# An attention and MLP block on one core: loads of turned score rows, issued one piece per step behind a one-element write

## The chip, the cores and the metric

The kernel runs on one core of one Trainium2 chip. The metric is device time in microseconds (us) of one execution. The engines are named as in the profile: PE is TensorE, DVE is VectorE, ACT is ScalarE, POOL is GpSimd, and SP is SyncE, which here only issues DMA transfers.

## What is computed

The input x has 2048 rows of 448 numbers in float32. The reference, cut to what matters:

```python
xn  = layernorm(x)
q, k, v = xn @ wq, xn @ wk, xn @ wv      # 16 heads of 28 for q, one shared head for k and v
p   = softmax(q_h @ k.T * 28 ** -0.5)    # 2048 x 2048 for each head h
att = concat_h(p @ v) @ wo
y   = layernorm(xn)
mlp = gelu(y @ w1 + b1) @ w2 + b2        # 448 -> 1792 -> 448
out = x + att + mlp
```

## The kernel before, in words

The kernel has three stages. The first (to about 90 us) normalises x, projects q, k and v, and stores q to DRAM (`qd`). The second (to about 483 us) computes the MLP, 56 slots of `slot`; its sums with x are stored to the DRAM tensor `ad` (line 635). The third, which this change is about, is attention. The order of the work of each engine is the order of the program, written by hand: a queue does its instructions one after another, and one that waits holds those behind it.

**Units and steps.** The 2048 query rows are cut into 4 chunks of 512 (index c), the 16 heads into 4 groups of 4 (index g). A unit u is one chunk and one group, so there are 16 units. A step takes two of the 16 blocks of 128 key rows (index kt = 0, 2, ... 14), so a unit has 8 steps and the loop at line 873 has 128. Each step runs a string of letters from `ORDERS` (line 29). The ones that matter here:

- `s`: one `score` (line 849): a matmul of keys with queries (line 857) and the exponential of ACT into a tile `p` (line 858).
- `m`: one piece of `max_stream` (line 506). For every head but the turned ones of the next item, score rows are computed once ahead of time the other way round (line 516) to find each row's maximum, which DVE reduces (line 517). The queries for it, `qm`, are loaded by `load_m` (lines 429 to 436) in four small transfers per head, issued in the attention stage by POOL (`loads = pool`, line 875) shortly before the head before is finished.
- `t` and `x`: `turned_scores` (line 544) and `turned_exp` (line 563), the same work for the fourth head of units 1 to 15, which is computed with the query rows on the partitions. Its exponentials are stored to DRAM, `td[u]`, by SP (line 571), four stores of 256 KB for each tile of 128 query rows. Most of these stores lie in the MLP stage. The rest are in the attention stage, four in a unit.
- `T`: `turn_blocks` (line 838): DVE transposes 32 x 32 blocks of a `half` (line 840) and so gives the step the two `p` tiles of the fourth head.
- `P`: `pv` (line 821), twice a step: the matmuls of one key block's `p` tiles with the values (line 826), 16 instructions a step.
- `n`: a step of `norm_jobs` (line 751), which divides the finished unit by its row sums. It is a chain across queues: ACT copies `po` to `oc` (line 754), POOL issues rc<-oc (766), DVE takes the reciprocal (769), POOL issues ld<-rc to DRAM (770) and, when that has landed, tr<-ld (774), then multiplies (778) and splits the product into `oth` and `otl` (784, 785).
- `o`: a step of the output projection, `o_jobs` (line 731), in units 5, 9 and 13 and at the end. It adds to a row tile `a` that `load_rows_of` (line 726) has loaded from `ad`, and SP stores the sum to the output (line 744).
- `e`: `load_max` (line 492): the row maxima of the next unit go through PE, ACT and DVE and then, as two small transfers of POOL (lines 503 and 504, xh<-mn), into the queries of that unit.

**The loads around the change.** A unit's turned rows come back from DRAM as two `half` tiles of 2 MB each, the first for kt < 8, the second for the rest. `load_d(u, h)` (line 707) takes a new tile from a ring of three and issues the load of one half as four transfers of 512 KB, one for each quarter of the partitions, on SP's queue. In the program it stands at kt = 10 and 14 of the unit before (kt = 0 and 4 in unit 0). A transfer of SP waits only for what it needs: the data it reads, and the last reader of the buffer it overwrites. Nothing else ties it to the step at whose head it stands. `load_rows_of` loads single rows of the sum (`a`, ring of four, 224 KB each) on the same queue: one tile at every second step of `o_wait` (line 861), and all four of the last chunk at the step 14 before the end (line 877).

The lines that place them, of the loop over steps:

```python
if n == len(steps) - 14:
    load_rows_of(NCH - 1, range(CT))
if u + 1 < NU and kt in ((10, 14) if u else (0, 4)):
    load_d(u + 1, kt in (4, 14))
...
if u + 1 < NU and kt < 8:
    load_q(u + 1, (kt // 2,))
```

Of the kernel before, what the change touches and what calls it, by code (L numbers as in the profile page):

```python
# [8 lines left out]
F32 = mybir.dt.float32  # L9
# [6 lines left out]
P = 128  # L16
S, D, H, DH, F = 2048, 448, 16, 28, 1792
NT = S // P
CT = 4
# [19 lines left out]
def block_kernel(ctx, tc, x, wq, wk, wv, wo, w1, b1, w2, b2, out):  # L39
    nc = tc.nc  # L40
    pe, act, dve, pool = nc.tensor, nc.scalar, nc.vector, nc.gpsimd
# [12 lines left out]
    def heads_of(u):  # L54
        return 3 if u in TURNED else 4
# [6 lines left out]
    td = {u: dram.tile([32, 8, 4 * CT, 256], F32, name=f"td{u}") for u in TURNED}  # L62
# [361 lines left out]
    NU = len(units)  # L424
# [49 lines left out]
    def load_q(u, blocks=range(4)):  # L474
        c, g = units[u]
        cols = slice(c * CW, (c + 1) * CW)
        if u < 2 and 0 in blocks:
            qst.append(xt_p.tile([P, 4, CW], F32R, name="xh"))
            pool.memset(f(qst[u]), 0.0)
        qs = qst[u % 2]  # L480
        for b in blocks:
            blk, i = ((1, 0), (2, 0), (0, 1), (3, 1))[b]
            nh = heads_of(u)
            src = qd[i][4 * DH * g:4 * DH * g + DH * nh, cols].rearrange("(j r) n -> r j n", r=DH)
            loads.dma_start(f(qs[32 * blk:32 * blk + DH, 0:nh, :]), src)  # L485
        qss[u] = qs
# [5 lines left out]
    def load_max(u):  # L492
        qs, mr = qss[u], mrs.pop(u)
        nh = heads_of(u)
        pm = mtile([nh * CT, P])
        pe.transpose(pm, mr[:, 0:nh * CT], ident)
        mn = keep.tile([4 * CT, 2, P], F32R, name="mn", bufs=1)[0:nh * CT]
        if u:
            act.activation(mn[:, 0, :], pm, AF.Copy, scale=-1.0)
        else:  # L500
            dve.tensor_scalar(mn[:, 0, :], pm, -1.0, 0.0, op0=ALU.mult, op1=ALU.add)
        dve.scalar_tensor_tensor(mn[:, 1, :], pm, -1.0, f(mn[:, 0, :]), op0=ALU.mult, op1=ALU.subtract)
        loads.dma_start(f(qs[60:61, 0:nh, :]), f(mn[:, 0, :]))
        loads.dma_start(f(qs[124:125, 0:nh, :]), f(mn[:, 1, :]))
# [58 lines left out]
    def turned_exp():  # L563
        if not exps:
            return
        u, t, raw, m3, h = exps.pop(0)
        rs = slice(2 * h, 2 * h + 2)
        act.activation(raw[:, rs], raw[:, rs], AF.Exp, bias=m3[:, 4:5], scale=1.0)  # L568
        if h == 1:
            for a in range(4):  # L570
                nc.sync.dma_start(td[u][:, :, 4 * t + a, :],
                                  raw[32 * a:32 * a + 32].rearrange("p r (h b) i -> p (r h) (b i)", h=2))
            stored[u] = t
# [96 lines left out]
    for n in range(len(mslots) + 2):  # L670
        c, ft = mslots[n] if n < len(mslots) else (NCH, n - len(mslots))
# [28 lines left out]
    att = ctx.enter_context(tc.tile_pool(name="att", bufs=2))  # L700
# [3 lines left out]
    wor = att.tile([P, NG, D], F32, name="wor", bufs=1)  # L704
    halves = {}

    def load_d(u, h):
        assert stored[u] == CT - 1
        halves[u, h] = att.tile([P, 4 * CT, 256], F32, name="half", bufs=3)
        for r in range(4):  # L710
            nc.sync.dma_start(halves[u, h][32 * r:32 * r + 32], td[u][:, 2 * r + h, :, :])

    woh = att.tile([P, NG, D], F32R, name="woh", bufs=1)
    wol = att.tile([P, NG, D], F32R, name="wol", bufs=1)
# [5 lines left out]
    def prep_wo(g):  # L720
        act.activation(woh[:, g, :], wor[:, g, :], AF.Copy)
        pool.tensor_sub(wol[:, g, :], wor[:, g, :], f(woh[:, g, :]))

    rows = {}

    def load_rows_of(c, tiles):
        for k in tiles:
            rows[c, k] = keep.tile([P, D], F32, name="a", bufs=4)
            nc.sync.dma_start(rows[c, k], ad[:, CT * c + k, :])

    def o_jobs(c, gs, tiles=range(CT)):
        last = NG - 1 in gs
        for k in tiles:
            po = mtile([P, D])
            ts = slice(k * P, (k + 1) * P)
            for g in gs:
                oth, otl = ots[c, g]
                pe.matmul(po, oth[:, ts], woh[:, g, :], start=(g == gs[0]), stop=False)
                pe.matmul(po, oth[:, ts], wol[:, g, :], start=False, stop=False)
                pe.matmul(po, otl[:, ts], woh[:, g, :], start=False, stop=(g == gs[-1]))  # L740
            a = rows[c, k]
            dve.tensor_add(a, a, po)
            if last:
                (nc.scalar if k % 2 and c == NCH - 1 else nc.sync).dma_start(ov[:, CT * c + k, :], a)
            yield
# [75 lines left out]
    def pv(u, kt):  # L821
        if kt == 0:
            pos[u] = op.tile([P, CW], F32, name="po")
        po = pos[u]
        for j in range(4):
            pe.matmul(po[32 * j:32 * j + 32, :], vs[:, kt, :], ps.pop((u, kt, j)),  # L826
                      start=(kt == 0), stop=(kt == NT - 1))
        if kt == NT - 1:
            if u == NU - 1:
                end_jobs(u, pos.pop(u))  # L830
                return
            side.add(norm_jobs(u, pos.pop(u)))
            side.step()
            c, g = units[u]
            if c < NCH - 1 and g == NG - 1:
                oside.add(o_wait(c, range(NG), range(CT)))

    def turn_blocks(u, kt):
        p = pair_of()
        dve.transpose(p.rearrange("p k (g j) -> p g k j", j=32),  # L840
                      halves[u, kt // 8][:, :, 32 * (kt % 8):32 * (kt % 8) + 64].rearrange("p g (k j) -> p g k j", j=32))
        ps[u, kt, 3], ps[u, kt + 1, 3] = p[:, 0], p[:, 1]
# [6 lines left out]
    def score(u, kt, j):  # L849
        if not halfway:  # L850
            p = pair_of()
            halfway.append(p[:, 1])
            p = p[:, 0]
        else:
            p = halfway.pop()
        s = mp.tile([P, CW], F32, name="m")
        pe.matmul(s, ks[:, kt * P:(kt + 1) * P], qss[u][:, j, :], start=True, stop=True)  # L857
        act.activation(p, s, AF.Exp, scale=SCALE)  # L858
        ps[u, kt, j] = p

    def o_wait(c, gs, tiles):
        for k in range(4):
            load_rows_of(c, tiles[k:k + 1])
            yield
            yield
        yield from o_jobs(c, gs, tiles)
# [6 lines left out]
    for n, (u, kt) in enumerate(steps):  # L873
        if n == 0:
            loads = pool
        if n == len(steps) - 14:
            load_rows_of(NCH - 1, range(CT))
        if u + 1 < NU and kt in ((10, 14) if u else (0, 4)):
            load_d(u + 1, kt in (4, 14))
        if 4 <= n < 4 + NG:  # L880
            prep_wo(n - 4)
        if u + 1 < NU and kt < 8:
            load_q(u + 1, (kt // 2,))
        jobs = [(u, kt + k, j) for k in range(2) for j in range(heads_of(u))]
        for what in ORDERS[u in TURNED][n % 2]:
            if what == "s":
                score(*jobs.pop(0))
            elif what == "m":
                if maxed < total - left + left * sum(weight[:n + 1]) / sum(weight):
                    maxed += mxs.step()  # L890
            elif what == "t":
                tq.step()
            elif what == "x":
                turned_exp()
            elif what == "T":
                if u in TURNED:
                    turn_blocks(u, kt)
            elif what == "e":
                if kt == (6 if u + 2 < NU else 10) and u + 1 < NU:
                    load_max(u + 1)  # L900
            elif what == "n":
                side.step()
            elif what == "o":
                if n == len(steps) - 5:
                    oside.add(o_jobs(NCH - 1, range(NG - 1)))
                oside.step()
            elif what == "P":
                assert not jobs
                for _ in range(BURST if n else 0):
                    pv(*pvq.pop(0))  # L910
# [29 lines left out]
```

## Time and profile before

| What | Value |
|---|---|
| median of the three runs | 1127.99 us (1127.91 to 1135.29) |
| the profiled execution | 1129.17 us |
| its span, first to last instruction | 1127.4 us |
| mean granted clock of PE over the span | 0.991 |
| DMA moved | 195.13 MB, mean 173 GB/s |
| `half` loads | 120 transfers of 512 KB, SP |
| stores of `td` | 240 transfers of 256 KB, SP |

The profile is one execution on the chip. Its head gives each engine's busy time; its other views group instructions by line, list who waited for whom, follow the chain that ended last, or show instructions in order of time. In those rows a name such as qm<-qd says what was written from what, an arrow with "<-" in a list of waits names the releaser, and brackets in the view by time hold the idle time before an instruction and its releaser. A stretch's row has the busy time and the number of instructions of each engine, then the clock granted to PE (1.00 is full), the mean busy share of the 16 DMA engines and what they moved. "Us to landing" is the time from a transfer's issue until its data are there; it is given for transfers that POOL issued. SPq and POOLq are the queues of those engines.

### The profile page before, as it was taken

The page shows a single profiled execution, that of the slowest core. Times are in us where ns is not written, and L with a number is a line of the kernel's source. Part 1 is how long each engine was busy: PE and PEld are TensorE (multiplying, and loading weights), DVE is VectorE, ACT ScalarE, POOL GpSimd, SP SyncE. Part 2 cuts the span into 40 slices and gives each one's busy share as a digit, 9 for nine tenths or more (in the row PEclk, how much of TensorE's full clock was granted, in tenths as well). Part 3 has the DMA queues.
Part 4 walks back from the last instruction along what each step waited for, and adds up shares of the span by engine and source line. Part 5 has one row for each costly group of instructions (what it writes and reads, how often), then busy time and mean ns, then how long its engine had stood idle before and what let it go on. Part 6 is the DMA issues. An engine that isn't in the chain of part 4 may idle for free.

```text
span 1127.4 us, 17253 instructions
## 1 busy us (share of the span) xinstructions
PE 1089.9 (97%) x5777; PEld 717.0 (64%) x5777; DVE 905.8 (80%) x1711; ACT 736.6 (65%) x1279; POOL 553.3 (49%) x683
## 2 busy tenths in 40 slices
PE   9999999999999999999999999999999989979988
PEld 8768878888888888854555456555455444545444
DVE  7789889888898988976889886888877968857734
ACT  6765655666667665578677765777755767745764
POOL 6357777778777777934324415333433333233120
PEclk9999999999999999999999999999999989989989
DMA  8775445777777777685787693979676957846910
GB/s 274 208 218 152 132 128 159 184 181 189 205 178 191 185 197 196 165 212 127 169 191 178 161 217 118 229 167 222 170 155 172 219 133 182 220 101 143 219 40 33
DMA packets 113669, 195.13 MB, mean 173 GB/s; under 512 B 17070, under 2 KB 96100, under 8 KB 109740
## 3 DMA queue, kind: packets, MB, share of 16 engines
q1 hardware_dynamic: 100972, 172.34, 61.3%
q0 software_dynamic: 11200, 21.10, 7.6%
q8 instruction: 46, 0.75, 0.3%
q10 hardware_dynamic: 1408, 0.57, 0.2%
q14 instruction: 43, 0.35, 0.1%
HBM read 115.22 MB, written 77.71 MB: 171 GB/s over the span
## 4 chain that ended last, share of the span: by engine, by line
PE 56%; DMA 21%; issue 8%; POOL 7%; DVE 5%; ACT 1%; SPq 1%; POOLq 0%; DVEq 0%; ACTq 0%
PE m L516 10%; PE po L826 9%; PE ph L179 9%; DMA ld<-rc 8%; PE m L857 8%; DMA qm<-qd 4%; PE m L550 4%; DMA tr<-ld 4%; PE m L627 3%; PE m L624 3%; PE m L630 3%; POOL qm L434 2%; DMA td<-raw 1%; POOL xh L485 1%; POOL tr L774 1%
## 5 line engine op out<-in xcount | busy, mean ns | idle before, releaser
L517 DVE TENSOR_REDUCE mx<-m 128x1 f32<-128x512 f32 x784 | 506.0, 680 | 111.4 <-PE m L516 102.8
L858 ACT ACTIVATE p<-m 128x512 f32<-128x512 f32 x784 | 402.9, 610 | 175.7 <-PE m L857 175.6
L516 PE MATMUL m<-ks,qm 128*128 128x512 f32 x784 | 324.3, 414 | 13.6 <-DMA qm<-qd 11.1
L857 PE MATMUL m<-xh,ks 128*128 128x512 f32 x784 | 260.8, 403 | 7.5 <-DMA xh<-mn 5.2
L826 PE MATMUL po<-p,vs 128*32 128x512 f32 x2048 | 249.7, 606 | 0.0
L516 PEld LDWEIGHTS m<-ks,qm 128*128 128x128 f32 x784 | 147.8, 188 | 134.9 <-ACT p L858 45.0
L857 PEld LDWEIGHTS m<-xh,ks 128*128 128x128 f32 x784 | 146.7, 190 | 56.6 <-ACT p L858 12.9
L551 DVE TENSOR_SCALAR_CACHE_REDUCE raw<-m 128x512 f32<-128x512 f32 x240 | 159.8, 689 | 18.5 <-DMA td<-raw 7.2
L840 DVE STREAM_TRANSPOSE p<-half 128x1024 f32<-128x1024 f32 x120 | 148.0, 1235 | 5.7 <-PE po L826 3.3
L568 ACT ACTIVATE raw<-raw,m 128x1024 f32<-128x1024 f32 x120 | 133.0, 1150 | 0.6 <-DVE m L557 0.6
L826 PEld LDWEIGHTS po<-p,vs 128*32 128x32 f32 x2048 | 54.1, 110 | 124.0 <-issue 118.3
L598 ACT ACTIVATE hx<-ph,b1t 128x512 f32<-128x512 f32 x56 | 38.6, 690 | 138.1 <-PE ph L184 138.1
L550 PE MATMUL m<-ks,q 128*128 128x512 f32 x240 | 95.6, 399 | 4.5 <-DVE raw L551 2.4
L613 POOL TENSOR_TENSOR hl<-hx,hh 128x512 fp32r<-128x512 f32 x56 | 73.4, 1311 | 35.4 <-ACT hh L611 35.4
L774 POOL DMA_DIRECT2D tr<-ld x56 | 28.1, 507 | 114.7 <-DMA ld<-rc 114.7
L630 PE MATMUL m<-w2h,hl 128*128 128x448 f32 x224 | 82.9, 370 | 0.3 <-POOL hl L613 0.3
L627 PE MATMUL m<-w2l,hh 128*128 128x448 f32 x224 | 81.7, 365 | 0.0
L624 PE MATMUL m<-w2h,hh 128*128 128x448 f32 x224 | 81.6, 364 | 0.0
L606 POOL TENSOR_TENSOR hx<-hx,hz 128x512 f32<-128x512 f32 x56 | 74.3, 1328 | 4.7
L601 POOL TENSOR_TENSOR hz<-hz,hx 128x512 f32<-128x512 f32 x56 | 72.6, 1296 | 4.7
L179 PE MATMUL ph<-xh,w1h 128*128 128x512 f32 x168 | 66.2, 394 | 0.0
L179 PE MATMUL ph<-xh,w1l 128*128 128x512 f32 x168 | 65.8, 391 | 0.0
(164 smaller groups left out, 1335.1 us busy)
## 6 DMA issues: line engine op xcount, KB each, us to landing
td<-raw SPq DMA_DIRECT2D x240, 256.0 KB
half<-td SPq DMA_DIRECT2D x120, 512.0 KB
xh<-qd POOLq DMA_DIRECT2D x60, 168.0 KB, 4.3
a<-in_A_x_dram SPq DMA_DIRECT2D x32, 224.0 KB
qd<-qe SPq DMA_DIRECT2D x24, 256.0 KB
qm<-qd POOLq DMA_DIRECT2D x108, 56.0 KB, 4.0
qm<-qd SPq DMA_DIRECT2D x88, 56.0 KB
ad<-a SPq DMA_DIRECT2D x16, 224.0 KB
```

The costliest lines, as they stand in the source:

```text
L179: pe.matmul(ps, w, v, start=(n == 0), stop=False)
L516: pe.matmul(pm, qm[:, t * P:(t + 1) * P], ks[:, n * CW:(n + 1) * CW], start=True, stop=True)
L517: dve.tensor_reduce(mx[:, CT * j + t, n:n + 1], pm, axis=AX.X, op=ALU.max)
L550: pe.matmul(sc, q3[i][:, t * P:(t + 1) * P], ks[:, n * CW:(n + 1) * CW], start=True, stop=True)
L551: dve.tensor_scalar(raw[:, :, 4 * n:4 * n + 4, :].rearrange("p r b i -> p b r i"), sc.rearrange("p (b r i) -> p b r i", r=4, i=32), SCALE, ...
L568: act.activation(raw[:, rs], raw[:, rs], AF.Exp, bias=m3[:, 4:5], scale=1.0)
L627: pe.matmul(m2[k], hh[:, ts], w2l[:, ft, :], start=False, stop=False)
L630: pe.matmul(m2[k], hl[:, ts], w2h[:, ft, :], start=False, stop=(ft == NF - 1))
L826: pe.matmul(po[32 * j:32 * j + 32, :], vs[:, kt, :], ps.pop((u, kt, j)), start=(kt == 0), stop=(kt == NT - 1))
L840: dve.transpose(p.rearrange("p k (g j) -> p g k j", j=32), halves[u, kt // 8][:, :, 32 * (kt % 8):32 * (kt % 8) + 64].rearrange("p g (k j) ...
L857: pe.matmul(s, ks[:, kt * P:(kt + 1) * P], qss[u][:, j, :], start=True, stop=True)
L858: act.activation(p, s, AF.Exp, scale=SCALE)
```

## The change

`load_d` takes an index i from 0 to 7 in place of a half. Each call issues one of the eight pieces of a unit, and before it DVE writes one element of that piece (a zero at its first partition and column, which the load then overwrites). The load writes the same element, so it cannot be issued before DVE has come to that write. The call stands at the head of every step of units 0 to 14, i = kt / 2. The rows of the sum get the same write. No transfer changes its size, its queue or its number.

```diff
-    def load_d(u, h):
+    def load_d(u, i):
         assert stored[u] == CT - 1
-        halves[u, h] = att.tile([P, 4 * CT, 256], F32, name="half", bufs=3)
-        for r in range(4):
-            nc.sync.dma_start(halves[u, h][32 * r:32 * r + 32], td[u][:, 2 * r + h, :, :])
+        h, r = divmod(i, 4)
+        if r == 0:
+            halves[u, h] = att.tile([P, 4 * CT, 256], F32, name="half", bufs=3)
+        part = halves[u, h][32 * r:32 * r + 32]
+        dve.memset(part[0:1, 0, 0:1], 0.0)
+        nc.sync.dma_start(part, td[u][:, 2 * r + h, :, :])
...
     def load_rows_of(c, tiles):
         for k in tiles:
             rows[c, k] = keep.tile([P, D], F32, name="a", bufs=4)
+            dve.memset(rows[c, k][0:1, 0:1], 0.0)
             nc.sync.dma_start(rows[c, k], ad[:, CT * c + k, :])
...
-        if u + 1 < NU and kt in ((10, 14) if u else (0, 4)):
-            load_d(u + 1, kt in (4, 14))
+        if u + 1 < NU:
+            load_d(u + 1, kt // 2)
```

## The prediction

> **What bounds the kernel now.** I read the page's head first, then its list of transfers, then TensorE's waits in the attention stage, then that stage in slices, and last the queues around the slices that lose time. All views here are of the kernel before. The head and two transfers of the page:
>
> ```profile
> span 1127.4 us, 17253 instructions
> PE 1089.9 (97%) x5777; PEld 717.0 (64%) x5777; DVE 905.8 (80%) x1711; ACT 736.6 (65%) x1279; POOL 553.3 (49%) x683
> ...
> td<-raw SPq DMA_DIRECT2D x240, 256.0 KB
> half<-td SPq DMA_DIRECT2D x120, 512.0 KB
> ```
>
> TensorE (PE) is busy for 1089.9 of 1127.4 us, so what can be won without taking work away is its 37.5 us of idle time and the time in which it runs slowly. The change touches only the attention loop, from about 483 us on. The view of who waited for whom, for PE in 480 to 1127 us (total, times, longest):
>
> ```profile
> PE m L516 <- DMA qm<-qd: 11.1, 3, 5.7
> PE m L857 <- DMA xh<-mn: 5.2, 1, 5.2
> PE m L516 <- ACT p L858: 1.4, 2, 0.8
> PE m L740 <- POOL otl L785: 1.4, 2, 0.7
> PE m L857 <- ACT p L858: 1.3, 2, 0.7
> PE m L738 <- POOL oth L784: 1.2, 1, 1.2
> ```
>
> And the first two of its lines in order of time (start, duration, in brackets the idle time before):
>
> ```profile
> 513.72 0.47 PE L516 MATMUL m<-ks,qm 128*128 128x512 f32 x1 [2.59 <-DMA qm<-qd]
> ...
> 912.88 0.77 PE L516 MATMUL m<-ks,qm 128*128 128x512 f32 x1 [2.86 <-DMA qm<-qd]
> ...
> 995.45 0.77 PE L516 MATMUL m<-ks,qm 128*128 128x512 f32 x1 [5.68 <-DMA qm<-qd]
> ...
> 1078.95 2.90 PE L857 MATMUL m<-xh,ks 128*128 128x512 f32 x6 [5.21 <-DMA xh<-mn]
> ```
>
> Four waits for small transfers of POOL's queue make 2.59 + 2.86 + 5.68 + 5.21 = 16.3 us. The four lines of waits for ACT and POOL add 1.4 + 1.4 + 1.3 + 1.2 = 5.3 us. Elsewhere PE runs nearly without a gap, as the last row of the next fence shows for units 2 and 3 together, whose 16 transposes on VectorE (DVE) are in the row behind it. The stretches are those after the four stalls, one within a burst of loads, and the two units (columns: us; busy us and count of PE, PEld, DVE, ACT, POOL; granted clock; DMA share; GB/s):
>
> ```profile
> 514.00:528.00 14.00, 14.00 (x82) 7.08 (x81) 8.22 (x15) 12.22 (x23) 7.52 (x12) 1.00 0.20 59
> ...
> 912.88:920.00 7.12, 7.12 (x25) 3.18 (x26) 2.12 (x5) 1.33 (x3) 5.12 (x7) 0.56 0.04 13
> 995.45:1002.00 6.55, 6.55 (x24) 2.87 (x25) 1.38 (x2) 2.49 (x5) 5.51 (x9) 0.57 0.30 86
> 1078.95:1084.00 5.05, 5.05 (x22) 2.32 (x22) 0.00 (x0) 3.05 (x6) 2.85 (x3) 0.60 0.00 0
> ...
> 574.00:596.00 22.00, 22.00 (x132) 10.99 (x131) 19.27 (x32) 15.05 (x32) 5.62 (x11) 1.00 1.02 231
> ...
> 564.65:636.31 71.66, 71.66 (x426) 36.36 (x425) 63.76 (x103) 54.16 (x106) 23.12 (x39) 1.00 0.77 183
> ```
>
> ```profile
> L840 DVE STREAM_TRANSPOSE p<-half x16: 1222/1235/1241, 564.7 to 632.2; 128x1024 f32<-128x1024 f32 x16
> ```
>
> After each of the three later stalls the granted clock is 0.56 to 0.60 for some microseconds. The loss is 7.12 x 0.44 + 6.55 x 0.43 + 5.05 x 0.40 = 8.0 us, counted as busy time. After the first stall it stays at 1.00.
>
> Why are the small transfers late? The DMA queue of SP, in order of time:
>
> ```profile
> 486.46 5.03 SPq L711 DMA_DIRECT2D half<-td  x8
> 527.69 3.28 SPq L571 DMA_DIRECT2D td<-raw  x4
> ...
> 570.56 3.42 SPq L571 DMA_DIRECT2D td<-raw  x4
> 574.08 7.70 SPq L711 DMA_DIRECT2D half<-td  x8
> 606.42 3.46 SPq L571 DMA_DIRECT2D td<-raw  x4
> ...
> 961.55 3.17 SPq L571 DMA_DIRECT2D td<-raw  x4
> ```
>
> Four stores of td come once a unit, 12 times from 527.69 to 961.55 us. Unit 2 begins at 564.7 us. In the program its loads of `half` stand at the sixth and eighth step, but nothing holds SP back: once past the stores of td it issues all eight within 7.7 us, 4 MB behind 1 MB. The row 574 to 596 shows the DMA engines full (1.02) for 22 us at 231 GB/s. What that does to the small transfers, from the groups of lines 770, 774, 434 and 503 in this order (ld<-rc, tr<-ld, qm<-qd, xh<-mn):
>
> ```profile
> DMA to landing us min/median/max: 1.7/10.1/13.0
> DMA to landing us min/median/max: 2.1/6.3/10.4
> DMA to landing us min/median/max: 2.0/4.0/17.6
> DMA to landing us min/median/max: 1.6/9.6/14.2
> ```
>
> POOL's queue outside a burst, and before the stall at 989.8 us:
>
> ```profile
> 700.67 2.01 POOL L774 DMA_DIRECT2D tr<-ld  x4 [1.45 <-DMA ld<-rc]
> ...
> 974.70 0.58 POOL L770 DMA_DIRECT2D ld<-rc  x1 [4.07 <-DVE mx L517]
> 984.91 2.04 POOL L774 DMA_DIRECT2D tr<-ld  x4 [9.64 <-DMA ld<-rc]
> 986.95 2.01 POOL L434 DMA_DIRECT2D qm<-qd  x4
> ```
>
> For the same 8 KB POOL idles 1.45 us where SP sends little and 9.64 us in a burst (1.7 and 10 us from issue to landing). POOL waits for them in order, so the next qm (or xh<-mn) is issued late, and then is slow itself.
>
> **The change part by part.** *Holding the loads of `half`.* No transfer is added or taken away: 120 of 512 KB before and after. One goes out per step, behind a write that DVE does at the head of that step. Units 2 and 3 have 16 steps in 71.66 us, 4.48 us each. At 231 GB/s a piece takes 524 KB / 231 = 2.3 us, so SP's queue is empty for about half of most steps. Ahead of a small transfer there is at most one piece, or once per unit a piece and the four stores of td (1.05 MB, 4.5 us). My estimate for ld<-rc is therefore 2 to 4.3 us as a rule in place of 10.
>
> What that does to each stall: before 989.8 us POOL is released at least 9.64 - 4.3 = 5.3 us sooner, so the four qm are issued from 981.6 to 983.6 us and, with their group's median of 4.0, are there near 987.6, before PE runs dry. The stall that ends at 912.88 is a qm's too, and so is the one that ends at 513.72, behind eight loads issued from 486.46 on; the longest landing of the group is 17.6 us. With a piece ahead instead of a burst each should land over 5 us sooner (17.6 against 4.0 + 6.8), more than the 2.86 and 2.59 lacking. The last stall is xh<-mn's, which stands behind tr<-ld, which waited for ld<-rc; from the chain that ended last:
>
> ```profile
> 1059.34 9.50 DMA ld<-rc
> ...
> 1071.13 7.54 DMA xh<-mn
> ```
>
> With 4.3 and about 5 us in their place it lands 9.50 - 4.3 + 7.54 - 5 = 7.7 us earlier, against 5.21 us of stall. So I take all four: 16.3 us, and 8.0 us of slow clock with them. The bounds of this term are 0 (the waits stay) and 24.3.
>
> The small waits for ACT and POOL (5.3 us) stand at the end of the same chain, since `oc`, `oth` and `otl` wait for tr<-ld. Some are the ordinary meeting of two engines. Between 0 and 5.3 I take the middle, 2.7.
>
> The clock term can be read against a rule. In the Trainium skill, TensorE: Matmul & The Clock Gate, section "The HAM clock gate", the clock halves after an idle window of about 3.4 us and returns after a busy window of about 3.4 us. By that figure, an estimate from the page, three stalls would cost 3 x 1.7 = 5.1 us instead of 8.0, and the time would be 2.9 us longer. The trace differs on both counts: a stall of 2.86 us was enough, and a mean of 0.56 over 7.12 us means some 6 us at half.
>
> *The 120 one-element writes, and 16 for the rows.* The nearest row is a small memset of this kernel, and what hides it is DVE's idle time beside it:
>
> ```profile
> L382 DVE MEMSET vs<- x4: 62/62/62, 22.0 to 63.7; 128x4 f32 x4
> ```
>
> ```profile
> DVE mx L517 <- PE m L516: 7.7, 14, 0.8
> ```
>
> 136 x 0.062 = 8.4 us of DVE. In units 2 and 3 DVE idles 71.66 - 63.76 = 7.9 us in 16 steps, 0.49 us a step, 7.7 of it waiting for PE (the second fence, waits of 564 to 637 us): a write of 0.06 us fits eight times. Nothing is queued behind it but DVE's own next instruction, and it has nothing to wait for: the last readers of the buffer are DVE's own transposes of an earlier step. Bounds 0 and, doubled for the signalling, 17 us; I take 1, since PE is what DVE waits for.
>
> *SP's queue.* A piece now waits for DVE, and behind it stand td's stores of the same step (which wait for ACT, later in that step), stores of out, and rows: all belong to this step or later ones, so nothing is held longer than its step. Cost nothing.
>
> *Later loads.* The fourth piece of a half is issued in step 4 of unit u and first read in step 1 of unit u + 1, five steps or 22 us later; the eighth in step 8, read in step 5 of the next, the same. Piece and td's stores take 2.3 + 4.5 + 2 = 9 us. Cost nothing.
>
> *Rows of the sum.* 16 loads of 224 KB are held to steps in the same way, and are used five or more steps on. Their write needs the store that last read the buffer, whose issue is at least six steps back. Cost nothing, gain nothing.
>
> Sum: -16.3 - 8.0 - 2.7 + 1.0 = -26.0 us. The profiled execution took 1129.17 us (span 1127.4), so 1103.2; the median of the three runs, 1127.99, is 1.2 lower: 1102.
>
> **The rivals.** *A piece hurts as much as a burst.* If a small transfer's delay comes from there being any traffic of SP's and not from how much is queued, spreading makes the traffic omnipresent: per unit 4.2 MB of pieces and 1 MB of stores take 5.2 / 0.231 = 23 us of 35.8, so two thirds of the chances to be late stay, and 24.3 us shrink by a third: 1128 - 8 = 1120. For it: the ld<-rc of 974.70 us landed within 10 us, well before the last of the transfers that delayed qm behind it. Against it: the row 1.7 / 10.1 / 13.0, where the fast ones stand in stretches with some SP traffic too. The Trainium skill says in DMA: Bandwidth & Descriptors, "Queues, rings and completion order", that an engine goes round its queues packet by packet; by that the length of SP's backlog should not matter, and this rival would hold. No run here separates the two yet. Chance 0.15.
>
> *The write waits for the piece before it (slower).* If the writes of one `half` tile were ordered one behind another, DVE would stand at the head of each step until the last piece has landed. That takes 2.3 + 2.0 = 4.3 us, within the step's 4.48 + 0.49; but with td's stores ahead 8.8, which is 3.8 too many, in the 12 units that store: +46 - 24 = +22, 1150 us. It decides from a landing above 5 us on. Against it: the eight loads of 486.46, four to a tile, were issued in 5 us while a burst lasts 22, so parts of a tile were not ordered. Chance 0.08.
>
> *The stalls have another cause, or are replaced by the next late thing*, so that no more than a few us come of it: 1125 to 1130. For it: in most units the same slow chain stalls nothing, so the stalls need a coincidence that may come again elsewhere. Chance 0.09.
>
> *DVE becomes the bound*: at 0.11 us a step on the path, 128 steps cost 14 us, 1115. Against it, 0.49 us idle. Chance 0.06.
>
> **How the numbers follow.** The forecast, 1094 to 1110, has 0.62: its high end keeps one stall with its slow clock (5.68 + 2.8), its low end lets all of the 5.3 us go and the writes cost nothing (3.6 in all), and leaves 4 us for work stretched around the stalls that no row prices. With the DVE case (1111 to 1116) and a piece as bad as a burst (1112 to 1124) that makes 0.83; the range 1094 to 1126 takes in these three. One per cent, 11.3 us, is about what a measurement of this kernel can tell from no change. Faster by more: 0.62 + 0.06 + a third of 0.15 = 0.73. Within: 0.10 + 0.09 = 0.19. Slower: 0.08.
>
> **What would show it.** Right: eight loads of `half` some 4.5 us apart in SP's queue; the DMA share no longer 1.0 for 20 us and then 0; ld<-rc at a median under 5 us; no wait of PE for qm or xh<-mn above 1 us; granted clock 1.00 up to the last unit; units without rows of the sum near 36 us throughout. Wrong: ld<-rc still near 10 us (the first rival), a wait of DVE in front of the new writes (the second), or new waits of PE for `mx` (the last).

## The result, and the profile after

The changed kernel takes 1098.1 us at the median of four runs (1096.8 to 1102.2), the kernel before 1130.6 us beside it (1127.9 to 1135.3). The ratio is 0.971, 95% interval 0.967 to 0.976. The forecast was 1102 us, 26 us below the 1128.0 that was the median of before at the time. Against the medians of this comparison the change saves 32.5 us.

The profiled execution of the changed kernel took 1102.2 us with a span of 1100.4. It is the longest of the four, and some 3.5 us of it were lost before the code that changed: in the projection stage the clock was 0.83 from 60 to 80 us (1.00 in the profile of before), and the first score's matmul starts at 487.47 instead of 483.98 us. From that matmul to the end the kernels take 1127.4 - 484.0 = 643.4 us before and 1100.4 - 487.5 = 612.9 us after. So the attention stage is 30.5 us shorter, and that is the number to explain. The rows of the two stretches, before and after (columns as in the prediction):

```profile
483.98:1127.40 643.42, 617.01 (x3565) 323.77 (x3565) 483.13 (x760) 436.77 (x845) 211.82 (x340) 0.98 0.70 165
```

```profile
487.47:1100.40 612.93, 607.30 (x3565) 321.17 (x3565) 488.23 (x895) 437.05 (x845) 212.26 (x340) 1.00 0.74 173
```

PE's idle time fell from 643.4 - 617.0 = 26.4 us to 612.9 - 607.3 = 5.6, which is 20.8 us less, and its busy time by 617.0 - 607.3 = 9.7 us for the same 3565 matmuls.

The waits of PE from 480 us on, complete, in the changed kernel (its lines 861 and 742 are 857 and 738 of before):

```profile
PE m L861 <- DVE half L713: 1.0, 1, 1.0
PE m L742 <- ACT oth L812: 0.9, 1, 0.9
```

No wait for qm, xh<-mn, ACT's `p`, `otl` or `oth` of the norm chain is left. These two stand at the first score and at the end, and were there before too (waits for `a` and for `oth`). The reason shows in the landings of the same four groups as in the prediction (ld<-rc, tr<-ld, qm<-qd, xh<-mn):

```profile
DMA to landing us min/median/max: 3.8/4.3/7.4
DMA to landing us min/median/max: 2.1/4.1/6.5
DMA to landing us min/median/max: 2.1/4.6/11.7
DMA to landing us min/median/max: 1.7/5.5/7.3
```

The median of ld<-rc fell from 10.1 to 4.3 us. Its minimum rose from 1.7 to 3.8: in no unit does it find the way free any more, and in none does it stand behind a whole burst. For qm the median did not fall (4.0 before, 4.6 now); its longest did, from 17.6 to 11.7 us. SP's queue and the stretches answer to those shown of before; the stretches are the one that was a burst, the one that was idle, two whole units, and nearly all of the stage:

```profile
571.27 3.65 SPq L571 DMA_DIRECT2D td<-raw  x4
575.01 29.05 SPq L714 DMA_DIRECT2D half<-td  x8
607.12 3.58 SPq L571 DMA_DIRECT2D td<-raw  x4
```

```profile
574.00:596.00 22.00, 22.00 (x132) 10.96 (x131) 19.51 (x38) 15.05 (x31) 8.79 (x14) 1.00 0.81 199
600.00:604.00 4.00, 4.00 (x26) 1.93 (x25) 3.66 (x7) 3.13 (x7) 0.00 (x0) 1.00 0.77 181
565.35:637.01 71.66, 71.66 (x426) 36.33 (x425) 64.48 (x119) 54.16 (x106) 28.25 (x46) 1.00 0.77 186
490.00:1052.00 562.00, 562.00 (x3294) 295.99 (x3296) 466.92 (x864) 407.57 (x789) 207.19 (x336) 1.00 0.79 186
```

Of the kernel before, the row of the idle stretch is:

```profile
600.00:604.00 4.00, 4.00 (x26) 1.94 (x25) 3.36 (x6) 3.25 (x8) 3.71 (x5) 1.00 0.01 3
```

The eight loads now take 29 us to issue where they took 7.7. The DMA share is 0.81 where it was 1.02, and 0.77 where it was 0.01. From 490 to 1052 us PE is busy in all of 562.00 us at a clock of 1.00. Units 2 and 3 take 71.66 us, to the hundredth what they took before: the steady state has not become faster, only the stalls are gone.

### The profile page after: what moved, and what is told of

The parts are those of the page before. It is cut to its first block, busy times and chain, and to the rows that moved or that the text cites. A ratio compares the mean times of both kernels' runs of the same rounds, so it can differ in the third digit from the quotient of the medians.

```text
span 1100.4 us, 17517 instructions
## 1 busy us (share of the span) xinstructions
PE 1082.9 (98%) x5777; PEld 716.4 (65%) x5777; DVE 911.2 (83%) x1847; ACT 736.6 (67%) x1279; POOL 553.6 (50%) x683
## 4 chain that ended last, share of the span: by engine, by line
PE 89%; DVE 5%; DMA 3%; SPq 1%; ACT 1%; issue 1%; POOL 0%; ACTq 0%; DVEq 0%; POOLq 0%
PE po L830 22%; PE m L516 18%; PE m L861 17%; PE ph L179 9%; PE m L550 5%; PE m L630 4%; PE m L627 4%; PE m L624 4%; DMA qd<-qe 1%; DMA qm<-qd 1%; PE m L742 1%; PE m L743 1%; PE m L744 1%; PE ph L182 1%; PE ph L184 1%; DVE mx L517 1%
## 5 line engine op out<-in xcount | busy, mean ns | idle before, releaser
L830 PE MATMUL po<-p,vs 128*32 128x512 f32 x2048 | 246.0, 598 | 0.0
L861 PEld LDWEIGHTS m<-xh,ks 128*128 128x128 f32 x784 | 144.7, 188 | 50.0 <-ACT p L862 12.8
L179 PE MATMUL ph<-xl,w1h 128*128 128x512 f32 x168 | 66.3, 395 | 0.0
```

Source lines behind the costliest of these rows:

```text
L179: pe.matmul(ps, w, v, start=(n == 0), stop=False)
```

## The experiments

Each kernel is timed against the kernel before on the same chip.

### The new places without the write

The change with both writes taken out, so that the loads stand one per step but nothing holds SP.

```diff
-        dve.memset(part[0:1, 0, 0:1], 0.0)
...
-            dve.memset(rows[c, k][0:1, 0:1], 0.0)
```

> The change without its one-element writes: the eight loads of a unit stand one per step in the program, but nothing holds SP to the step. Theory 1 (small transfers are late by what SP has queued in front of them, and it is the hold that keeps this short): SP runs ahead as before, the eight loads go out within 8 to 10 us behind td's stores, ld<-rc stays near 9 to 10 us at the median, PE waits for qm or xh<-mn again; time 1120 to 1132 us. Theory 2 (it is the new place in the program, earlier in the unit and evenly spread, that helps): 1096 to 1104 us with ld<-rc near 4 us.

Measured: 1113.2 us, ratio 0.984 (0.981 to 0.987). The time lies between the ranges of the two theories. ld<-rc stayed at 9.6 us at the median, as theory 1 had it. SP's queue in two views, all eight loads of unit 2 and those that it had issued by 590 us:

```profile
577.97 25.46 SPq L713 DMA_DIRECT2D half<-td  x8
```

```profile
577.97 7.89 SPq L713 DMA_DIRECT2D half<-td  x6
```

The six pieces that stand behind td's stores in the unit go out in 8 us. The last two are the next unit's first; they come 16 us later, since the tile that they overwrite is still being read by DVE. So the ring of three tiles holds a part of the loads even without a write, and six in place of eight run together. Three waits of PE stay (3.91 and 6.17 us for qm, 0.47 for xh<-mn). Place alone gave a little more than half of the gain (18.9 us; the loads of `half` held and spread, in half_only below, gave 33.7 against the same runs of the kernel before), and the burst that is left still hurts.

### The write at the old places

```diff
-        if u + 1 < NU:
-            load_d(u + 1, kt // 2)
+        if u + 1 < NU and kt in ((10, 14) if u else (0, 4)):
+            for r in range(4):
+                load_d(u + 1, 4 * (kt in (4, 14)) + r)
```

> The writes kept, but the pieces at the old places: four at the sixth and four at the eighth step of a unit, each piece behind its own write. A burst is then 2 MB (9 us at 231 GB/s) instead of 4 MB behind 1 MB, and lies after the step in which ld<-rc is issued. Theory 1: ld<-rc lands in 2 to 4.5 us; of the stalls one at most is left; 1097 to 1108 us. Theory 2 (even spreading is what is needed): ld<-rc short, but qm and xh<-mn late behind 2 MB as they were; 1110 to 1125 us.

Measured: 1116.3 us, ratio 0.986 (0.984 to 0.989), as theory 2 had it. This run changes the explanation, since ld<-rc is now quick in every unit (1.7 us at the median, 2.0 at most) and PE waits all the same. The landings of ld<-rc, and POOL's queue before the wait in unit 13:

```profile
DMA to landing us min/median/max: 1.7/1.7/2.0
```

```profile
963.77 0.58 POOL L774 DMA_DIRECT2D ld<-rc  x1 [4.08 <-DVE mx L517]
965.80 2.06 POOL L778 DMA_DIRECT2D tr<-ld  x4 [1.45 <-DMA ld<-rc]
967.85 2.01 POOL L434 DMA_DIRECT2D qm<-qd  x4
978.81 1.26 POOL L782 TENSOR_TENSOR oc<-oc,tr 128x512 f32<-128x512 f32 x1 [8.95 <-DMA tr<-ld]
```

```profile
984.22 0.76 PE L516 MATMUL m<-ks,qm 128*128 128x512 f32 x1 [5.40 <-DMA qm<-qd]
```

The qm were issued from 967.85 to 969.86 us, and PE ran dry at 978.8, nine microseconds later; they came after 14. Four loads of `half` go out from 964.17 us, before them, and four from 972.72, while they are under way. So the norm chain is not the only way to a stall: a qm that is issued in good time is late by itself when 2 to 4 MB go with it. As in the kernel before, the other two waits end at 514 us (4.29) and at 1065.58 (2.82). For the last the profile names no releaser; the second transfer of xh<-mn, issued at 1055.30 us, had landed at 1065.49.

### One half of the change at a time

The loads of `half` held and the rows not, and the other way round: the write for the rows alone, in the kernel before.

```diff
half_only: the change without
-            dve.memset(rows[c, k][0:1, 0:1], 0.0)
...
rows_only: the kernel before with
+            dve.memset(rows[c, k][0:1, 0:1], 0.0)
```

> The loads of half are held and spread as in the change; the rows of the sum have no write. Both theories: 16 loads of 224 KB matter little, 1096 to 1102 us, no different from the change. If the rows carried a part of the gain, 1105 us or more.

Measured: 1098.5 us, ratio 0.971 (0.969 to 0.974). The whole gain is in the loads of `half`.

> The kernel before, with the write only in front of the 16 loads of rows. Both theories: the bursts of half stay, 1124 to 1132 us. One thing could differ: in the last chunk SP no longer issues the four rows ahead of their step, which delays the loads of half behind them; if the late stalls depend on that, 5 us in either direction.

Measured: 1137.5 us, ratio 1.005 (1.003 to 1.007), half a per cent slower. PE waits in the same four places as before, for 4.52, 2.09, 6.46 and 6.74 us. All but the second are longer than in the profile of before (2.59, 2.86, 5.68 and 5.21). The profile is of the fastest of its ten runs (1132.0 us), so it need not show what the median lost. The cause stays open.

### How much may be in front: 1, 2 and 4 MB

Three kernels with everything held, which differ only in how many pieces go out together: two every second step, four at the first and fifth step, all eight at the fifth.

```diff
-        if u + 1 < NU:
-            load_d(u + 1, kt // 2)
held_twos:
+        if u + 1 < NU and kt % 4 == 0:
+            for r in range(2):
+                load_d(u + 1, kt // 2 + r)
held_fours:
+        if u + 1 < NU and kt % 8 == 0:
+            for r in range(4):
+                load_d(u + 1, kt // 2 + r)
held_all_at_8:
+        if u + 1 < NU and kt == 8:
+            for i in range(8):
+                load_d(u + 1, i)
```

> The change, but two pieces every second step instead of one every step: 1 MB in front of a small transfer at most (4.5 us at 231 GB/s) where no store of td is near. Theory 1a (what makes PE wait is the number of bytes that SP has put in front of a single qm or xh<-mn; bursts of 2 MB left two or three waits, 0.5 MB none, and the slack of those transfers is over 5 us): no wait of PE for them, 1096 to 1102 us. Theory 1b (any clumping costs in proportion): half of what bursts of 2 MB cost, 1104 to 1110 us.

> The change, but four pieces at the first and four at the fifth step of a unit: 2 MB at a time (9.1 us at 231 GB/s), with 9 us between two bursts. So far bursts of 0.5 and 1 MB left no wait of PE, while pieces held in fours at the sixth and eighth step (two bursts that run into each other, 4 MB in 18 us) left three. Theory 1a (a wait comes when the bytes in front take longer than the slack of the transfer; qm that were issued in time had 13 us: issued by 896.6, needed at 910.0 us in the kernel before): qm lands within 4 + 9 = 13 us, so at most one wait is left; 1097 to 1105 us. Theory 1b (cost in proportion to the clump): half way between 1 MB and the old places, 1106 to 1112 us.

> The change, but all eight pieces at the fifth step of a unit, held there: 4 MB (18 us) in one burst, after ld<-rc has been issued. Theory 1a: qm behind it lands after up to 4 + 18 = 22 us, more than its slack of 13 us, so waits of PE for qm or xh<-mn of 3 to 8 us each come back although ld<-rc is quick; 1110 to 1128 us. Rival (holding as such is what helps, whatever the size): 1096 to 1102 us.

| In one go | Time, us | Ratio to before (95%) | Waits of PE for qm and xh<-mn |
|---|---|---|---|
| 0.5 MB (the change) | 1098.1 | 0.971 (0.967 to 0.976) | none |
| 1 MB | 1098.2 | 0.971 (0.967 to 0.975) | none |
| 2 MB | 1108.5 | 0.977 (0.971 to 0.983) | 5.1 us, and 0.3 |
| 4 MB | 1151.0 | 1.015 (1.009 to 1.020) | 11.5 us in three and 7.7; also 13.9 us for ACT |

Up to 1 MB there is no difference, as theory 1a had it. At 2 MB it had at most one wait; the profile shows one of 5.1 us and one of 0.3. The median, 1108.5 us, lies in the range of theory 1b and outside that of 1a, but the four runs lie between 1100 and 1114 us, so that time does not tell the two apart. At 4 MB the held kernel is slower than the kernel before and lies outside the range of both: the write by itself is no cure. The longest waits of PE there, and POOL's queue in unit 2:

```profile
PE m L516 <- ACT p L862: 13.9, 7, 3.7
PE m L516 <- DMA qm<-qd: 11.5, 3, 7.6
PE m L861 <- issue: 7.7, 1, 7.7
```

```profile
579.98 0.58 POOL L774 DMA_DIRECT2D ld<-rc  x1 [1.17 <-DVE rc L773]
584.40 2.01 POOL L778 DMA_DIRECT2D tr<-ld  x4 [3.85 <-DMA ld<-rc]
586.40 2.01 POOL L434 DMA_DIRECT2D qm<-qd  x4
600.50 1.28 POOL L782 TENSOR_TENSOR oc<-oc,tr 128x512 f32<-128x512 f32 x1 [12.08 <-DMA tr<-ld]
```

For the third line the view names no releaser ("issue"). It ends at 1100.80 us, and the second transfer of xh<-mn, issued at 1085.62, landed at 1100.70, so that it is counted as a wait for xh<-mn.

The burst starts at 580.28 us, so ld<-rc slips through and tr<-ld meets all of it: POOL stands for 12 us, `oc` is not free for the next unit, ACT waits for it in order, and PE for ACT's exponentials. Size is not all of it, since the three kernels differ in the place of their bursts too: here tr<-ld lands after 12.1 us at the median, while the kernel with the write at the old places, which sends the same 4 MB in two bursts at the sixth and eighth step, has it at 2.2 us and takes 1116.3 us. Size and place were not varied one at a time. In the 2 MB kernel the one wait has the path that the prediction described: ld<-rc is behind a burst, so that POOL is held and issues qm late.

```profile
960.88 0.58 POOL L774 DMA_DIRECT2D ld<-rc  x1 [4.08 <-DVE p L844]
971.17 2.04 POOL L778 DMA_DIRECT2D tr<-ld  x4 [9.71 <-DMA ld<-rc]
973.21 2.02 POOL L434 DMA_DIRECT2D qm<-qd  x4
```

### Twelve more writes a step

```diff
         dve.memset(part[0:1, 0, 0:1], 0.0)
+        for _ in range(12):
+            dve.memset(spare, 0.0)
```

> The change with 12 more one-element writes of VectorE in each step of units 0 to 14, so 120 x 12 x 0.059 = 85 us more of its time. Theory (the writes are free because VectorE idles some 0.45 us a step and waits for PE): 0.71 us a step is 0.26 us more than the idle time in the 88 steps of units 1 to 11, so 1098 + 23 = 1121 us, between 1110 and 1130, and waits of PE for what VectorE releases. Rival (VectorE already sets the pace, the writes of the change cost what they last): 1098 + 85 = 1175 or more, over 1160 us. Rival (writes overlap with what is beside them and cost nothing at all): 1097 to 1102 us.

Measured: 1172.3 us, ratio 1.036 (1.032 to 1.041). That is 74 us more than the change, outside the range of the theory and inside that of the first rival. DVE in order of time (the writes to `spare` are the added ones):

```profile
609.54 0.06 DVE L714 MEMSET half<- 1x1 f32 x1
609.65 1.19 DVE L716 MEMSET spare<- 1x1 f32 x11
610.88 0.69 DVE L517 TENSOR_REDUCE mx<-m 128x1 f32<-128x512 f32 x1
```

```profile
L847 DVE STREAM_TRANSPOSE p<-half x16: 1222/1235/1242, 575.2 to 654.9; 128x1024 f32<-128x1024 f32 x16
```

A write is busy for 59 ns, but eleven take 1.19 us: 0.11 us from one to the next. Theory and rival both counted only the 59. Twelve are therefore 1.3 us a step; in the last row 16 transposes begin over 79.7 us, where units 2 and 3 of before needed 67.5 (564.7 to 632.2), which is 12.2 / 15 = 0.8 us a step. So about 0.5 us of the 1.3 were free, the idle time that the prediction had read off (0.49), and the rest came out one to one. The view of waits shows none of DVE in units 2 and 3 any more, so there it does set the pace. Against the change, units 1 to 4, 6 to 8, 10 and 11 lose 6.2 to 6.5 us each (0.8 us a step), unit 0 loses 8.0, unit 12 4.6, and units 5 and 9, where PE has the output projection besides, 1.6 and 1.9; together with the last units that makes the 74 us. If no part of a write were hidden, 120 times 1.3 us would have been added, 156 us. So the one write of the change fits, with some four times its cost in reserve.

### The change in the last units only

The loads that stand in units 0 to 8 as before (`old_d` is the load of a piece without the write), those in units 9 to 14 as in the change, the rows held throughout.

```diff
-        if u + 1 < NU:
-            load_d(u + 1, kt // 2)
+        if u >= 9:
+            if u + 1 < NU:
+                load_d(u + 1, kt // 2)
+        elif kt in ((10, 14) if u else (0, 4)):
+            for r in range(4):
+                old_d(u + 1, 4 * (kt in (4, 14)) + r)
```

> The kernel before up to unit 8, the change in units 9 to 14 (the rows of the sum held throughout). By the sum of the prediction three stalls lie there: 2.86 + 5.68 + 5.21 us and 8.0 us of slow clock. Theory 1: these vanish, the first stall and the small waits of units 3 to 9 stay; 1102 to 1109 us. Rival (the gain is spread over all units, since every unit has bursts): nine fifteenths of it stay away, 1114 to 1120 us.

Measured: 1112.6 us, ratio 0.984 (0.980 to 0.989), between the two. The transposes show why, first of the kernel before and then of this one, for units 10 to 15:

```profile
L840 DVE STREAM_TRANSPOSE p<-half x48: 1191/1235/1246, 878.1 to 1112.3; 128x1024 f32<-128x1024 f32 x48
```

```profile
L850 DVE STREAM_TRANSPOSE p<-half x48: 1202/1235/1246, 885.6 to 1098.5; 128x1024 f32<-128x1024 f32 x48
```

From the start of unit 10 to the end of the kernel it is 1127.4 - 878.1 = 249.3 us before and 1113.7 - 885.6 = 228.1 here: 21.2 us less, where the prediction's three stalls and their slow clock are 13.75 + 8.0 = 21.75. That part is as predicted. What was not expected is that units 0 to 9 took 7.2 us longer: 1.6 us of PE's idle time and 5.6 of its busy time. Their waits are those of before, but some are longer (3.87 us for the first qm, 2.12 for `oth` in unit 9), and the clock fell behind both and once more near 686 us, where in the profile of before it stayed at 1.00. The profile is of the slowest of its four runs (1115.6 us), and the rows are held here, which alone cost half a per cent above; what part of the 7.2 us each has was not separated. Runs of the kernel before, beside it, lie between 1125.7 and 1135.7 us.

### A third buffer for qm

The kernel before, with qm loaded one head earlier in the attention stage, and nothing held.

```diff
...
-                        qms.append(load_m(*heads[h + 1]))
+                        if not since:
+                            qms.append(load_m(*heads[h + 1]))
+                            if ring:
+                                since.append(h + 2)
+                                ring.extend(qmt[(h + k) % 2] for k in range(2))
+                        if since and h + 2 < len(heads):
+                            qms.append(load_m(*heads[h + 2]))
...
+    ring.append(att.tile([P, CW], F32R, name="qm2", bufs=1))
...
```

> The kernel before, bursts and all, but qm in the attention stage with a third buffer, loaded one head (16 pieces of the maxima, about 12 us) earlier; nothing is held. Theory 1 (a stall is a small transfer that comes after its deadline; there is nothing else in a burst that costs time): PE no longer waits for qm; the wait for xh<-mn (5 us and its slow clock) and the small waits for ACT and POOL stay; 1108 to 1116 us. Rival (POOL's queue, held behind tr<-ld, is what makes qm late, an earlier place does not help): 1122 us or more.

Measured: 1127.2 us, ratio 0.996 (0.993 to 0.999), which is in the range of the rival and 11 us above that of theory 1. Its longest waits of PE:

```profile
PE m L867 <- DMA xh<-mn: 5.2, 1, 5.2
PE m L524 <- DMA xh<-mn: 4.1, 1, 4.1
PE m L524 <- ACT p L868: 4.0, 5, 1.2
PE m L867 <- ACT p L868: 1.9, 3, 0.7
PE m L750 <- POOL otl L795: 1.7, 3, 0.7
PE m L748 <- POOL oth L794: 1.5, 1, 1.5
```

The stalls at 912 and 995 us are gone, so an earlier issue does help qm. (The second line is the stall at 514 us, before the third buffer comes into use. The view names xh<-mn, but a qm issued at 495.43 us landed at 514.54, just before PE went on.) That contradicts the rival's reason, although the time is the one it gave. Two things ate up the gain. The waits for ACT and POOL grew from 5.3 to 9.1 us. And the stall at 514 us, which the third buffer does not touch, was 4.12 us instead of 2.59, with a mean clock of 0.59 in the 7.3 us behind it, where the profile of before had 1.00; that is some 4.5 us. That the bursts now hit the next transfer that has a deadline, the tr<-ld of the norm chain (7.5 us at the median, 6.3 before), fits the longer waits for ACT and POOL, but no run isolates it. Theory 1 was right that an earlier qm is no longer waited for, and wrong in taking the other waits as given.

## Why the prediction was right, point by point

*The hold spreads the loads*: right. Eight loads in 29 us and the DMA share even, as forecast.

*ld<-rc at 2 to 4.3 us*: 3.8 to 7.4, median 4.3, so the upper end of the estimate is the middle of what was measured. The estimate took an empty path in half of each step; the DMA share is 0.79 over the stage. That this is the reason is not shown.

*Four stalls, 16.3 us, and 8.0 us of slow clock*: right. None is left, and PE is at full clock from 490 to 1052 us. From unit 10 on, where the three stalls with a slow clock lie, PE's busy time fell by 7.4 us (230.8 to 223.4), against a forecast of 8.0. The last-units run puts 21.2 us against 21.75 for waits and clock of these three together.

*Their mechanism*: right as to the cause, too narrow as to the path. The prediction explained the stall at 989.8 us by POOL being held behind ld<-rc, and took a late landing of qm itself for the two before it. The old places with the write had every ld<-rc at 1.7 us and a stall at the same place. Either path is enough, late issue behind the chain or a late landing of the transfer itself, and it takes shorter bursts to close both.

*Small waits, 2.7 of 5.3 us*: mis-sized. All 5.3 went. The prediction's 26.0 is 4.5 below the 30.5 us that the stage lost: 2.6 here; 1.0 for the writes, of which the rows show no sign; 2.3 us of PE's busy time that went before unit 10, at a clock of 1.00 in both kernels, for which the prediction had left room at the low end of its range and no term; against that 0.6 us less than forecast from the slow clock, and 0.8 us that the end of the kernel, behind the last wait for `oth`, took longer. Why PE's busy time fell by the 2.3 us is open.

*The writes are hidden*: right. They last 59 ns (0.11 us from one to the next, where twelve more stand behind each), and DVE waits in front of none of them; a step has some 0.5 us to spare.

*Rows: nothing gained or lost*: right beside the held loads (1098.5 and 1098.1 us). In the kernel before, the same write cost half a per cent, which the prediction did not foresee.

*The rivals.* That a piece hurts as much as a burst is refuted: 0.5 and 1 MB leave no wait, 2 MB one above 1 us, 4 MB many. With one and the same hold, qm's longest landing was 11.7 us at 0.5 MB, 10.7 at 1 MB, 12.8 at 2 MB and 18.0 at 4 MB, so the length of SP's backlog does matter when it is long. By the packet-by-packet rule of the Trainium skill (DMA: Bandwidth & Descriptors, "Queues, rings and completion order") the length of SP's backlog should not matter; the measurement decides against reading the rule that far. That a write waits for the piece before it is refuted by the view of DVE's waits, which has none in front of the writes. That new waits take the stalls' place did not happen. DVE became the bound with twelve more writes a step; from the 0.5 us that were free, four should still fit.

## What to carry to other kernels

A queue that only issues transfers runs ahead to wherever its next wait is, so a load's place in the program is not its time; look at the queue in order of time before trusting it. If small transfers with deadlines share the DMA engines with large loads, find out how much may be in front of them (here, at the steps tried, 1 MB was free and 2 MB was not) and tie each piece to a step by a dependency on an engine with idle time to spare. Spreading is what helps: the same tie in front of one big burst made the kernel slower than no tie at all.

## What the runs showed of the hardware

- Whether PE's clock falls behind a wait is not told by the wait's length alone. In the kernel before it is at half (0.50) in three stretches of the attention stage, which begin at 912.33, 994.25 and 1076.17 us, inside the waits:

```profile
912.33:919.15 6.82, 6.27 (x22) 2.52 (x23) 1.38 (x2) 0.74 (x2) 4.27 (x5) 0.50 0.02 7
994.25:1001.07 6.82, 5.62 (x22) 2.43 (x22) 1.38 (x2) 2.17 (x4) 6.38 (x9) 0.50 0.22 66
1076.17:1082.99 6.82, 4.04 (x14) 2.22 (x18) 0.00 (x0) 3.05 (x6) 3.16 (x3) 0.50 0.07 17
```

  The starts lie 81.92 us apart, which is twelve times the length of a stretch (6.83). In the kernel without the write the clock is at half for 3.41 us behind the first qm's stall. That stall of 3.91 us is over before the clock falls, so that the first matmul behind it still takes 0.47 us:

```profile
516.21 0.47 PE L516 MATMUL m<-ks,qm 128*128 128x512 f32 x1 [3.91 <-DMA qm<-qd]
```

```profile
512.30:516.21 3.91, 0.01 (x1) 0.03 (x1) 0.91 (x3) 1.09 (x3) 0.00 (x0) 1.00 0.43 90
516.55:519.96 3.41, 3.41 (x16) 1.19 (x18) 1.39 (x2) 1.55 (x3) 1.13 (x2) 0.50 0.03 5
```

  These figures fit a clock that changes only at fixed marks 3.41 us apart (6.83 is twice that), so that it matters where a wait falls between them. In the 4 MB kernel it fell behind a wait of 2.44 us that ended at 643.65 (0.50 from 645.05 to 648.47), and not behind one of 2.87 that ended at 1062.49 (1.00 up to 1072). In the kernel before it fell with a wait of 2.86 us and not after one of 2.59. The Trainium skill (TensorE: Matmul & The Clock Gate, "The HAM clock gate") has a free-running window of about 3.4 us, and the 3.41 of the traces agrees; it has the clock fall after at least one idle window, and waits of 2.44 and 2.86 us are shorter than that.
- One-element writes of VectorE, one behind another without a wait, follow each other every 0.11 us, while the busy column gives 59 ns (the run with twelve more writes).
